# Linear attention with a highway layer: token rows by DMA transposes in the last four steps, seven shared PSUM banks, and a new order of the work

## The chip, the cores and the metric

The kernel runs on one core of one Trainium2 chip. Its time is device microseconds from launch to end. A profile is one profiled execution; it gives a span (first to last recorded work) and that execution's own time, which is a little longer than its span.

The engines are named as in the profile: PE is TensorE (matmuls), with PEld its weight loads; DVE is VectorE; ACT is ScalarE; POOL is GpSimd; SP is SyncE, which here issues nearly all DMAs. Each engine takes its instructions in the order in which they were written, and waits at an instruction whose input is not there yet.

## The reference

Four batches of 768 positions with 8 heads of 64 go through causal linear attention with a decay per head; the result, as 3072 token rows of 512, goes through a highway layer.

```python
for b in range(nb):                       # blocks of 64 positions
    intra = einsum('bhic,bhjc->bhij', qb, kb) * Dmask        # Dmask: lam ** (i - j), 0 above the diagonal
    intra = einsum('bhij,bhjd->bhid', intra, vb)
    inter = einsum('bhid,bhde->bhie', qb * lam_pow, kv_state)
    out[:, :, sl] = intra + inter
    kv_state = lam_block * kv_state + einsum('bhsd,bhse->bhde', kb * rev_pow, vb)
x = out as rows [3072, 512]
H = maximum(x @ w_h, 0);  T = sigmoid(x @ w_t + b_t)
return T * H + (1 - T) * x
```

## The kernel before

The 3072 tokens are worked in 12 steps of 256. A step n is a third of one batch; it has two blocks (0 and 1) of 128 tokens, which lie on partitions 0 to 63 and 64 to 127 of the q, k and v tiles. The decay is put into q (times a power of lam) and into v (times its inverse), so the mask is a plain triangle (`tri`) and the state `kv` only adds up in one PSUM bank of its own.

The work is a list of tokens, `PLAN`. It is the order in which the program is written, and so the order on every engine and in SP's DMA queue; `@DVE`, `@ACT`, `@POOL` choose an engine, the digits behind `=` the PSUM banks. For a step the tokens are:

- `Lq`, `Lk`, `Lv`: loads by SP, two of 256 KB for each. `CQ`, `CK`, `CV`: casts to bf16 with the powers (L231 to L247). `CQ` of either half of the q tile needs both q loads of the step.
- `TQ`, `TK`: q and k turned by TensorE, in eight whole 128x128 transposes each (L264) or in sixteen half ones (L267). `EB`: the result copied from PSUM to `kqT` by ACT or DVE.
- `SP.n.0`, `SP.n.1` (in step 0 `S` and `U`): scores (L285) and state updates (L290). `M`: the mask, four per step, on DVE (L338). `KE`: the state copied out for the next block.
- `I`, `A`: what the state gives (L353) and what the block itself gives (L363), added in one bank; `D` copies it to `xT`, with features on partitions and tokens along the row.
- `XT`: TensorE turns `xT` of both blocks to token rows, eight 128x128 transposes (L375) into one bank, and `XE` copies them to `xr` (L378). `xr` has three buffers.
- The highway layer, per block: `F.n.b.0` is x @ w_h and `F.n.b.1` is x @ w_t (L394, four matmuls of 512 columns each), where `PB` has put the bias into the gate's bank before (L388, ACT). Then `H`: max(h, 0) - x on DVE (L402); `G`: sigmoid on ACT (L407); `X`: the product on DVE (L410); `AD`: plus x, on POOL (L413); `ST`: the store by SP. In step 11 each of these is split into two halves of 256 columns.

`Z` tokens (L428) and `ZT` (L424) are matmuls on zeros, written into banks whose contents nothing reads; they stand where TensorE has little else to do, most of them before the first loads have arrived. The kernel uses eight PSUM banks: one for `kv`, five (`pb`) for all passing results and two (`pt`) for the gates only, which take turns.

Of the kernel before, what the change touches and what calls it, by code (L numbers as in the profile page):

```python
# [22 lines left out]
EB.1.0@ACT D.0.0@ACT Z.5=2 SP.1.0=341 WC.0.0.1@POOL D.0.1@DVE KE.1.0@ACT Z.2=2 I.1.1=0 M.1.0.0@DVE I.1.0=1 CK.2.2@ACT
SP.1.1=2 M.1.1.1@DVE WC.0.1.0@ACT M.1.1.0@DVE Lq.3.0 Lq.3.1 M.1.0.1@DVE TK.2.1=43 A.1.1 A.1.0 CV.2.2@POOL TQ.2.1
XT.0=2 WC.0.0.0@DVE D.1.0@DVE EB.2.0@ACT XE.0@ACT Lk.3.0 Lk.3.1 D.1.1@ACT Lv.3.0 Lv.3.1 WC.1.0.0@POOL F.0.1.0=1 Lk.4.0
KE.1.1@ACT EB.2.1@DVE F.0.0.0=4 H.0.1@DVE WC.1.0.1@ACT WC.1.1.1@ACT Lq.4.1 Lq.4.0 Lk.4.1 Lv.4.1 Lv.4.0 H.0.0@DVE
I.2.0=1 SP.2.0=023 XT.1=4 WC.1.1.0@DVE F.0.1.1 M.2.1.1@DVE F.0.0.1 KE.2.0@ACT M.2.0.0@DVE XE.1@ACT M.2.1.0@DVE
G.0.1@ACT I.2.1=4 CQ.3.2@POOL Lq.5.1 Lq.5.0 Lk.5.0 X.0.1@DVE G.0.0@ACT SP.2.1=0 F.1.0.0=3 M.2.0.1@DVE Lk.6.0 A.2.1
Lk.5.1 Lv.5.1 X.0.0@DVE H.1.0@DVE CK.3.2@POOL A.2.0 Lv.5.0 CV.3.2@POOL PB.1.0@ACT D.2.1@ACT TK.3.0=02 TQ.3.0 D.2.0@DVE
EB.3.1@DVE F.1.0.1 AD.0.0@POOL XT.2=1 PB.2.0@ACT F.2.0.0=2 EB.3.0@DVE SP.3.0=043 G.1.0@ACT XE.2@ACT X.1.0@DVE  # L30
PB.1.1@ACT KE.3.0@ACT F.2.0.1 H.2.0@DVE Lk.6.1 M.3.1.0@DVE Lq.6.1 Lq.6.0 CK.4.2@ACT I.3.1=2 G.2.0@ACT SP.3.1=0
M.3.0.0@DVE CQ.4.2@POOL M.3.1.1@DVE F.2.1.0=1 M.3.0.1@DVE H.2.1@DVE TQ.4.0=43 Lv.6.1 TK.4.0 A.3.1=0 A.3.0 F.1.1.1
KE.3.1@ACT EB.4.0@DVE CV.4.2@POOL EB.4.1@ACT Lk.7.0 Lv.6.0 SP.4.0=341 D.3.1@ACT AD.0.1@POOL D.3.0@DVE X.2.0@DVE
CQ.5.2@POOL M.4.1.0@DVE M.4.1.1@DVE M.4.0.0@DVE XT.3=0 F.3.0.0=2 KE.4.0@ACT AD.2.0@POOL CV.5.2@POOL AD.1.0@POOL
XE.3@ACT F.3.1.0=3 I.4.0=1 I.4.1=0 CK.5.2@ACT H.3.0@DVE SP.4.1=4 F.1.1.0=2 Lq.7.1 Lk.8.1 Lq.7.0 H.3.1@DVE M.4.0.1@DVE
KE.4.1@DVE PB.2.1@ACT G.1.1@ACT CK.6.2@ACT Lv.7.1 TQ.5.0=34 TK.5.0 CQ.6.2@POOL F.2.1.1 EB.5.1@ACT H.1.1@DVE G.2.1@ACT
EB.5.0@DVE X.1.1@DVE PB.3.1@ACT A.4.1 A.4.0 D.4.1@ACT X.2.1@DVE Lk.7.1 SP.5.0=432 F.3.1.1 KE.5.0@ACT D.4.0@ACT
M.5.1.1@DVE G.3.1@ACT TK.6.1=30 TQ.6.1 PB.3.0@ACT Lk.8.0 Lv.7.0 I.5.0=1 M.5.0.0@DVE M.5.1.0@DVE Lq.8.1 I.5.1=4
X.3.1@DVE SP.5.1=2 EB.6.0@ACT PB.4.1@ACT F.3.0.1 M.5.0.1@DVE Lq.8.0 ST.0.1 Lv.8.0 Lq.9.1 Lq.9.0 A.5.1 G.3.0@ACT A.5.0
EB.6.1@DVE AD.1.1@POOL CV.6.2@POOL D.5.1@ACT Lk.9.0 CQ.7.2@POOL SP.6.0=023 X.3.0@DVE Lq.10.1 Lv.8.1 D.5.0@ACT  # L40
PB.4.0@ACT CK.7.2@POOL F.4.1.1 ST.0.0 M.6.1.0@DVE M.6.1.1@DVE M.6.0.0@DVE ST.1.0 Lq.10.0 XT.4=1 AD.2.1@POOL F.4.1.0=0
CV.7.2@POOL Lk.10.1 Lk.10.0 Lv.9.1 G.4.1@ACT ST.2.0 Lk.9.1 TK.7.0=24 KE.6.0@ACT TQ.7.0 XE.4@ACT H.4.1@DVE I.6.1=3
EB.7.1@DVE SP.6.1=1 X.4.1@DVE AD.3.1@POOL AD.3.0@POOL F.4.0.1 XT.5=0 Lv.9.0 F.4.0.0=4 CQ.9.2@POOL CQ.8.2@POOL
CK.8.2@ACT G.4.0@ACT EB.7.0@ACT M.6.0.1@DVE XE.5@DVE A.6.1=1 A.6.0 D.6.0@ACT CV.8.2@POOL D.6.1@ACT H.4.0@DVE
KE.6.1@DVE F.5.1.0=0 X.4.0@DVE AD.4.0@POOL PB.5.1@ACT PB.6.1@ACT SP.7.0=142 KE.7.0@ACT XT.6=3 XE.6@ACT H.5.1@DVE
F.5.1.1 M.7.0.0@DVE M.7.1.0@DVE M.7.1.1@DVE I.7.1=2 I.7.0=0 SP.7.1=1 F.6.1.0=3 M.7.0.1@DVE TK.8.0=14 G.5.1@ACT TQ.8.0
F.6.1.1 X.5.1@DVE A.7.1 EB.8.1@DVE KE.7.1@ACT PB.5.0@ACT H.6.1@DVE A.7.0 EB.8.0@ACT AD.4.1@POOL ST.4.0 G.6.1@ACT
SP.8.0=314 D.7.1@ACT D.7.0@ACT F.5.0.1 X.6.1@DVE M.8.0.0@DVE M.8.1.0@DVE KE.8.0@ACT PB.6.0@ACT M.8.1.1@DVE F.5.0.0=2
AD.5.1@POOL I.8.0=4 Lv.11.0 I.8.1=3 SP.8.1=0 F.6.0.1 ST.1.1 Lv.10.0 Lv.10.1 M.8.0.1@DVE G.5.0@ACT CK.9.2@ACT
CK.10.2@ACT CV.9.2@POOL H.5.0@DVE X.5.0@DVE A.8.1 A.8.0 TQ.9.0=20 D.8.1@DVE AD.5.0@POOL Lk.11.1 ST.3.0 Lk.11.0  # L50
D.8.0@ACT TK.9.0 F.6.0.0=1 EB.9.1@ACT XT.7=3 ST.2.1 EB.9.0@DVE SP.9.0=204 G.6.0@ACT PB.8.0@ACT XE.7@ACT H.6.0@DVE
X.6.0@DVE XT.8=1 F.8.0.1 ST.3.1 F.8.0.0=3 M.9.0.0@DVE M.9.1.0@DVE XE.8@ACT CQ.10.2@POOL M.9.1.1@DVE KE.9.0@DVE
# [428 lines left out]
```

## Time and profile before

| | |
|---|---|
| time, median of 3 runs | 103.66 us (103.03 to 103.72) |
| profiled execution, its own time | 104.03 us |
| its span | 102.3 us |
| busy: PE / DVE / ACT / POOL | 91.1 / 81.2 / 75.2 / 76.0 us |
| granted TensorE clock | 0.998 |
| moved by DMA | 27.56 MB, 269 GB/s over the span |

In a list of windows each row is a stretch of the span in us, its length, and then for PE, PEld, DVE, ACT and POOL the busy time with the number of instructions; behind them the granted clock, the share of time in which the 16 DMA engines were busy, and GB/s. The chain of waits has a start, a duration, an engine, the tile that is written and a line. A group of instructions has its line, engine, operation, tiles, shapes and count, then busy time and mean ns of one, then the engine's idle time before them and what ended it. Busy times of an engine's neighbouring instructions overlap a little, so that four masks in a row took 2.49 us, about 620 ns each, where their mean is 684.

### The profile page before, as it was taken

The numbers are of one execution on the slowest core, as the hardware profiler recorded it, in microseconds if no ns is written. First come the engines' busy times: TensorE is split into PE (matmuls) and PEld (weight loads), VectorE is DVE, ScalarE is ACT, GpSimd is POOL, SyncE is SP. The second block draws the span as 40 slices with busy tenths as digits, with TensorE's granted clock in tenths as the row PEclk, the third lists the DMA queues.
The fourth block names the chain that finished last, engine by engine and source line by source line (L and its number), as shares of the span: only waits on it lengthen the run. The fifth ranks groups of instructions, "written<-read, shape, count | busy, mean of one in ns | idle before, by whom it ended". The sixth has DMA issues, their size and how long they took to land.

```text
span 102.3 us, 4447 instructions
## 1 busy us (share of the span) xinstructions
PE 91.1 (89%) x1883; PEld 56.2 (55%) x1907; DVE 81.2 (79%) x143; ACT 75.2 (73%) x124; POOL 76.0 (74%) x67
## 2 busy tenths in 40 slices
...
GB/s 8 255 294 357 347 360 366 375 397 351 281 286 345 334 285 290 258 347 331 302 342 267 373 333 330 314 243 274 357 378 245 68 143 103 109 2 148 252 272 55
DMA packets 36870, 27.56 MB, mean 269 GB/s; under 512 B 1777, under 2 KB 33009, under 8 KB 36850
## 3 DMA queue, kind: packets, MB, share of 16 engines
...
q10 hardware_dynamic: 146, 0.01, 0.1%
...
## 4 chain that ended last, share of the span: by engine, by line
PE 74%; DVE 11%; ACT 6%; issue 4%; POOL 0%; DVEq 0%; POOLq 0%
PE pt L394 18%; PE pb L394 18%; PE pb L285 7%; PE pb L428 6%; DVE m L338 6%; PE pb L363 6%; PE pb L375 5%; PE pb L353 5%; PE pb L267 5%; ACT xr L110 2%; ACT kqT L110 2%; PE kv L290 2%; PE pb L264 1%; DVE gx L410 1%; ACT pt L407 1%
## 5 line engine op out<-in xcount | busy, mean ns | idle before, releaser
L338 DVE TENSOR_TENSOR m<-pb,tri 128x512 bf16<-128x512 f32 x48 | 30.7, 684 | 5.2 <-PE pb L285 4.5
L239 POOL TENSOR_TENSOR qb<-qf,pow_q 128x1024 bf16<-128x1024 f32 (+1 forms) x13 | 22.6, 1747 | 11.4 <-DMA qf<-in_q_dram 9.9
L413 POOL TENSOR_TENSOR o<-gx,xr 128x512 f32<-128x512 bf16 x22 | 25.3, 1156 | 7.4 <-DVE gx L410 6.0
L394 PEld LDWEIGHTS <-xT 128*128 128x128 bf16 x208 | 18.1, 98 | 15.5 <-issue 0.4
L394 PE MATMUL pt<-w_b,xT 128*128 128x512 bf16 (+1 forms) x90 | 23.5, 361 | 1.5 <-issue 0.6
L394 PE MATMUL pb<-w_b,xT 128*128 128x512 bf16 (+1 forms) x97 | 23.7, 362 | 0.5 <-issue 0.2
L246 POOL TENSOR_TENSOR vs<-vf,pow_v 128x1024 bf16<-128x1024 f32 x10 | 19.1, 1905 | 1.8 <-DMA vf<-in_v_dram 1.2
L407 ACT ACTIVATE pt<-pt 128x512 f32<-128x512 f32 (+1 forms) x26 | 14.4, 554 | 4.5 <-PE pt L394 4.3
L410 DVE TENSOR_TENSOR gx<-pt,hm 128x512 bf16<-128x512 f32 x22 | 15.1, 687 | 3.2 <-ACT pt L407 2.7
L388 ACT ACTIVATE pt<-bt_all 128x512 f32<-128x512 f32 x24 | 14.4, 604 | 3.7 <-DVE gx L410 3.6
L402 DVE SCALAR_TENSOR_TENSOR hm<-pb,xr 128x512 bf16<-128x512 f32 x22 | 15.0, 685 | 2.0 <-ACT xr L110 1.8
L110 ACT ACTIVATE kqT<-pb 128x1024 bf16<-128x1024 bf16 x12 | 12.3, 1024 | 4.7 <-PE pb L264 3.4
L285 PE MATMUL pb<-kqT 64*64 64x128 bf16 x384 | 14.4, 220 | 0.6 <-DVE kqT L112 0.3
L285 PEld LDWEIGHTS <-kqT 64*64 64x64 bf16 x384 | 11.2, 105 | 2.3 <-ACT xT L110 0.8
L110 ACT ACTIVATE xr<-pb 128x1024 bf16<-128x1024 bf16 x11 | 11.2, 1024 | 1.6 <-PE pb L375 1.4
L290 PE MATMUL kv<-vs,kb 64*64 64x64 bf16 x320 | 11.8, 193 | 0.0
L110 ACT ACTIVATE xT<-pb 128x512 bf16<-128x512 f32 x18 | 10.2, 595 | 1.3 <-PE pb L363 1.3
L290 PEld LDWEIGHTS <-kb 64*64 64x64 bf16 x320 | 9.8, 107 | 0.4 <-issue 0.4
L428 PE MATMUL pb<-blank,id 128*128 128x512 bf16 x28 | 8.9, 467 | 0.2 <-issue 0.2
L363 PE MATMUL pb<-m,vs 64*64 64x128 bf16 x384 | 7.9, 219 | 1.1 <-issue 0.6
L363 PEld LDWEIGHTS <-vs 64*64 64x64 bf16 x384 | 6.0, 106 | 5.3 <-issue 5.0
L112 DVE COPY kqT<-pb 128x1024 bf16<-128x1024 bf16 x12 | 8.1, 683 | 0.4 <-PE pb L267 0.3
...
## 6 DMA issues: line engine op xcount, KB each, us to landing
...
w_f<-in_moe_w_h_dram SPq DMA_DIRECT2D x2, 512.0 KB, 6.9
w_f<-in_moe_w_t_dram SPq DMA_DIRECT2D x2, 512.0 KB, 8.0
out_dram<-oh SPq DMA_DIRECT2D x4, 128.0 KB, 2.4
lam_all<-in_lam_dram ACTq DMA_DIRECT2D x1, 4.0 KB, 3.1
```

Of the source, the lines that this page charges most:

```text
L110: A.activation(dst, src, AF.Copy)
L239: ENG[eng].tensor_tensor(new(("qb", n), [128, 4, 4, D])[:, :, ys], in0=get("qf", n)[:, ys].rearrange("p y (i d) -> p i y d", i=4), in1=pow ...
L246: ENG[eng].tensor_tensor(new(("vs", n), [128, H, J, D])[:, hs], in0=get("vf", n)[:, hs].rearrange("p h (j d) -> p h j d", j=J), in1=pow_v[ ...
L285: T.matmul(get("s", n, e, hp // 2)[half(b), hp % 2, j, :], lhsT=keys(n, e, hp, j, b), rhs=queries(n, e, hp, b), start=True, stop=True)
L290: T.matmul(kv[half(e), hp], lhsT=get("kb", n)[half(b), j, 2 * hp + e, :], rhs=get("vs", n)[half(b), 2 * hp + e, j, :], start=first, stop=T ...
L338: V.tensor_tensor(new(("m", n, e, u), [128, 2, J, C]), in0=get("s", n, e, u), in1=tri[:, None].to_broadcast([128, 2, J, C]), op=ALU.mult)
L363: T.matmul(get("o", n, b)[half(e), hp, :], lhsT=get("vs", n)[half(b), 2 * hp + e, j, :], rhs=get("m", n, e, u)[half(b), hp % 2, j, :], sta ...
L394: T.matmul(t, lhsT=get("xT", n, b)[:, kc, :], rhs=w_b[w][:, kc, cs], start=(w == 0 and kc == 0), stop=(kc == KC - 1), skip_group_check=boo ...
L407: A.activation(t, t, AF.Sigmoid)
L410: V.tensor_tensor(small("gx", n, b, p), in0=get("t", n, b)[:, cols(p)], in1=get("hm", n, b, p), op=ALU.mult)
L413: ENG[eng].tensor_tensor(small("o", n, b, p, F32), in0=get("gx", n, b, p), in1=get("xr", n)[:, b, cols(p)], op=ALU.add)
L428: T.matmul(banks[bk[0]], lhsT=id128, rhs=blank, start=True, stop=True)
```

## The change

For steps 8 to 11 the tokens `XT` and `XE` are gone. In their place `XD.n.b` has SP issue a DMA that transposes `xT` of one block (128x512 bf16, 128 KB) straight into `xr`, eight DMAs in all. Steps 0 to 7 still use TensorE. The two gate banks are gone as banks of their own: seven `pb` banks serve all results and the gates, and `PB` names a bank. The `o` tiles, which wait for their store, are twelve instead of eight, and `kqT` has three buffers instead of two. The scores' matmuls open a bank only with the first of a half, which changes no instruction's size. Step 0's q and k are turned in half transposes rather than whole ones (steps 1, 2 and 6 keep whole ones). `PLAN` is a new list: the same operations but for those named, in another order, some on other engines.

```diff
-BUFS = dict(kf=5,qf=5,vf=5,kb=3,qb=3,vs=3,kqT=2,m=8,xT=6,xr=3,hm=4,gx=4,hmh=4,gxh=4,ss=4,o=8,oh=4,tb=2)
+BUFS = dict(kf=5,qf=5,vf=5,kb=3,qb=3,vs=3,kqT=3,m=8,xT=6,xr=3,hm=4,gx=4,hmh=4,gxh=4,ss=4,o=12,oh=4)
...
-    banks = [ps.tile([128, 512], F32, name=f"pb{i}") for i in range(5)]
-    gates = [ps.tile([128, DM], F32, name=f"pt{i}") for i in range(2)]
+    banks = [ps.tile([128, 512], F32, name=f"pb{i}") for i in range(7)]
...
+    def turn_dma(n, b):
+        nc.sync.dma_start_transpose(out=new(("xr", n), [C, 2, DM])[:, b].rearrange("p (j f) -> p j f", f=128),
+                                    in_=get("xT", n, b).rearrange("p j t -> p (j t)"))
...
-    def preset(n, b):
-        made["t", n, b] = gates[gate_turn[0] % 2]
-        gate_turn[0] += 1
-        A.activation(get("t", n, b), bt_all, AF.Copy)
+    def preset(n, b, bk):
+        A.activation(bank(("t", n, b), bk[0], [C, DM]), bt_all, AF.Copy)
...
+        "XD": lambda a, e, bk: turn_dma(*a),
-        "XT": lambda a, e, bk: turn(*a, bk), "XE": lambda a, e, bk: evac_x(*a, e), "PB": lambda a, e, bk: preset(*a),
+        "XT": lambda a, e, bk: turn(*a, bk), "XE": lambda a, e, bk: evac_x(*a, e), "PB": lambda a, e, bk: preset(*a, bk),
```

Of the list, the first line and the line where the last step's `XD` stands show what kind of change it is:

```diff
-Lq.0.0 Lk.0.0 ZT Z.11=3 B=0 Lq.0.1 Lk.0.1 Lv.0.0 Lv.0.1 CQ.0.1@POOL Lq.1.0 Lv.1.1 CK.0.0@DVE CK.0.1@POOL Lq.1.1
+Lq.0.1 Lq.0.0 CQ.0.1@POOL CQ.0.0@POOL Lk.0.0 Lk.0.1 CK.0.0@DVE ZT Z.6=6 TQ.0.0=01 Lv.0.0 Lv.0.1 CK.0.1@ACT Lq.1.0
...
+F.10.0.0=3 PB.10.1@ACT=5 PB.11.0@ACT=0 F.10.1.0=1 F.10.1.1 H.10.0@DVE G.10.1@ACT ST.8.0 ST.7.0 ST.6.1 XD.11.1
```

The start, on POOL and after the constants. `qb` is the cast q, `kb` the cast k, `vs` the cast v; `qf_69` is q of step 0 and `qf_70` q of step 1. Before:

```order
L239 TENSOR_TENSOR qb_170<-qf_69,pow_q 128x4x128
L112 CAST kb_174<-kf_64 128x4x2x64
L239 TENSOR_TENSOR qb_184<-qf_70,pow_q 128x4x128 x2
L112 CAST kb_241<-kf_65 128x4x2x64
L239 TENSOR_TENSOR qb_337<-qf_71,pow_q 128x1024
```

And now:

```order
L238 TENSOR_TENSOR qb_156<-qf_69,pow_q 128x4x128 x2
L238 TENSOR_TENSOR qb_265<-qf_70,pow_q 128x4x128
L112 CAST kb_307<-kf_65 128x4x2x64
L238 TENSOR_TENSOR qb_265<-qf_70,pow_q 128x4x128
L245 TENSOR_TENSOR vs_317<-vf_75,pow_v 128x512 x2
```

Both halves of the first q are now cast on POOL, one after the other, where DVE had one; the second half of k of step 0 goes from POOL to ACT, and v of step 1 from DVE to POOL.

The end, on DVE, from the last mask (`m`) on. `hm`/`hmh` are `H`, `gx`/`gxh` are `X`, `oh` is an `AD` of half a row, `xT` is `D`. Before, where `xr_647` is step 10 and `xr_819` step 11:

```order
L338 TENSOR_TENSOR m_483<-pb_145,tri 128x512
L402 SCALAR_TENSOR_TENSOR hm_568<-pb_146,xr_647 128x512
L410 TENSOR_TENSOR gx_663<-pt_148,hm_568 128x512
L402 SCALAR_TENSOR_TENSOR hm_577<-pb_146,xr_647 128x512
L410 TENSOR_TENSOR gx_698<-pt_149,hm_577 128x512
L402 SCALAR_TENSOR_TENSOR hmh_2457<-pb_146,xr_819 128x256
L402 SCALAR_TENSOR_TENSOR hmh_2459<-pb_143,xr_819 128x256
L410 TENSOR_TENSOR gxh_2475<-pt_148,hmh_2459 128x256
```

And now, where `xr_570` is step 9, `xr_590` step 10 and `xr_855` step 11:

```order
L344 TENSOR_TENSOR m_492<-pb_153,tri 128x512
L401 SCALAR_TENSOR_TENSOR hm_648<-pb_149,xr_570 128x512
L409 TENSOR_TENSOR gx_788<-pb_151,hm_648 128x512
L401 SCALAR_TENSOR_TENSOR hm_650<-pb_148,xr_570 128x512
L112 CAST xT_782<-pb_152 128x512
L409 TENSOR_TENSOR gx_963<-pb_147,hm_650 128x512
L401 SCALAR_TENSOR_TENSOR hm_595<-pb_150,xr_590 128x512
L409 TENSOR_TENSOR gx_685<-pb_153,hm_595 128x512
L401 SCALAR_TENSOR_TENSOR hm_606<-pb_148,xr_590 128x512
L401 SCALAR_TENSOR_TENSOR hmh_2461<-pb_150,xr_855 128x256
L409 TENSOR_TENSOR gx_743<-pb_152,hm_606 128x512
```

Behind the last mask DVE had the `H` and `X` of step 10 and the halves of step 11; now it has those of step 9 too, and one `D` of step 11.

SP's queue, late. `out_dram<-o` is a store, `DMA_TRANSPOSE` an `XD`. Before, the last rows are stores only:

```order
L416 DMA out_dram<-o_83 128x512
L416 DMA out_dram<-o_86 128x512
L416 DMA out_dram<-o_82 128x512
L416 DMA out_dram<-o_84 128x512
L416 DMA out_dram<-oh_87 128x256
```

And now, from the transposes of step 10 to those of step 11:

```order
L380 DMA_TRANSPOSE xr_590<-xT_564 128x4x128
L380 DMA_TRANSPOSE xr_590<-xT_554 128x4x128
L415 DMA out_dram<-o_83 128x512
L415 DMA out_dram<-o_81 128x512
L415 DMA out_dram<-o_79 128x512
L380 DMA_TRANSPOSE xr_855<-xT_779 128x4x128
L380 DMA_TRANSPOSE xr_855<-xT_782 128x4x128
L415 DMA out_dram<-o_85 128x512
```

Three stores (of `AD.8.0`, `AD.7.0`, `AD.6.1`) stand ahead of the two transposes of step 11, and the rest of the stores behind them.

More of the change, by code (lines that the diff above doesn't have):

```diff
@@ L23 @@
[L23 to L52, printed above, removed]
```

96 lines of the change are left out of this document (62 added, 34 removed).

## The prediction

> **What bounds the kernel now.** I read the page's first part, the chain of waits, and then busy time in windows cut where the work changes.
>
> ```profile
> PE 91.1 (89%) x1883; PEld 56.2 (55%) x1907; DVE 81.2 (79%) x143; ACT 75.2 (73%) x124; POOL 76.0 (74%) x67
> PE 74%; DVE 11%; ACT 6%; issue 4%; POOL 0%; DVEq 0%; POOLq 0%
> 0.00:9.60 9.60, 8.17 (x24) 2.92 (x25) 4.29 (x15) 4.35 (x7) 4.17 (x13) 1.00 0.74 219
> 9.60:17.10 7.50, 6.16 (x146) 4.58 (x147) 5.85 (x11) 4.04 (x6) 2.61 (x3) 1.00 1.11 356
> 17.10:25.40 8.30, 7.37 (x201) 5.45 (x203) 6.89 (x12) 6.15 (x10) 5.79 (x5) 1.00 1.08 375
> 25.40:89.98 64.58, 61.91 (x1435) 38.25 (x1452) 57.27 (x94) 54.43 (x89) 56.86 (x39) 1.00 0.88 276
> 89.98:97.80 7.82, 7.50 (x84) 4.98 (x84) 5.80 (x13) 5.86 (x12) 5.91 (x6) 1.00 0.43 161
> 97.80:102.30 4.50, 0.00 (x0) 0.00 (x0) 1.14 (x3) 0.37 (x1) 0.67 (x1) 0.96 0.38 133
> ```
>
> In the long middle (25.40 to 89.98) PE is busy 61.91 of 64.58 us, and the chain is 74% PE: less work for PE is time there, as long as nobody else takes over. DVE is next with 57.27 (89%). The middle has 2.67 us of PE idling to win at most. Before 25.40 PE waits for others; after 97.80 it has ended.
>
> ```profile
> 9.73 0.91 PE pb L264 x16
> 11.90 0.44 PE pb L285 x13
> 12.43 0.67 DVE m L338
> 16.44 0.61 DVE kqT L112
> 17.10 0.22 PE pb L285 x2
> 29.25 0.57 PE pb L267 x32
> 81.76 0.86 PE pt L394 x4
> 87.88 0.45 PE pb L375 x8
> 89.76 0.23 PE pb L285 x6
> 90.95 0.57 PE pb L363 x32
> 97.33 0.45 PE pt L394 x4
> 97.80 0.38 ACT pt L407
> 98.20 0.44 DVE gxh L410
> 98.66 0.43 DVE oh L413
> ```
>
> These pieces of the chain give the prices on PE: q and k of a step turned whole 0.91 us (x16) or in halves 0.57 (x32), a block of the highway layer 0.86, `XT` 0.45, an intra pair 0.57, half a block 0.45. They also give the marks: first scores at 11.90, step 1's first scores at 17.10, the last scores' end at 89.98 (T below), the last matmul's end at 97.78, the last `AD`'s end at 99.09. The last store and the end take 102.30 - 99.09 = 3.21.
>
> **The change part by part. Sums first.** Without `XT` in four steps PE loses 4 x 0.45 = 1.80, and without the whole transposes of step 0 another 0.34. What the other engines lose or get:
>
> ```profile
> L338 DVE TENSOR_TENSOR m<-pb,tri 128x512 bf16<-128x512 f32 x48 | 30.7, 684 | 5.2 <-PE pb L285 4.5
> L402 DVE SCALAR_TENSOR_TENSOR hm<-pb,xr 128x512 bf16<-128x512 f32 x22 | 15.0, 685 | 2.0 <-ACT xr L110 1.8 <-PE pb L394 0.2
> L410 DVE TENSOR_TENSOR gx<-pt,hm 128x512 bf16<-128x512 f32 x22 | 15.1, 687 | 3.2 <-ACT pt L407 2.7
> L402 DVE SCALAR_TENSOR_TENSOR hmh<-pb,xr 128x256 bf16<-128x256 f32 x4 | 1.6, 418 | 0.2 <-ACT xr L110 0.2
> L410 DVE TENSOR_TENSOR gxh<-pt,hmh 128x256 bf16<-128x256 f32 x4 | 1.7, 425 | 0.6 <-ACT pt L407 0.3
> L112 DVE CAST xT<-pb 128x512 bf16<-128x512 f32 x6 | 4.1, 684 | 0.9 <-PE pb L363 0.9
> L112 DVE COPY xr<-pb 128x1024 bf16<-128x1024 bf16 x1 | 0.7, 681 | 0.0
> L110 ACT ACTIVATE xr<-pb 128x1024 bf16<-128x1024 bf16 x11 | 11.2, 1024 | 1.6 <-PE pb L375 1.4
> L110 ACT ACTIVATE kb<-kf 128x1024 bf16<-128x1024 f32 x7 | 7.3, 1065 | 0.0
> L413 POOL TENSOR_TENSOR o<-gx,xr 128x512 f32<-128x512 bf16 x22 | 25.3, 1156 | 7.4 <-DVE gx L410 6.0
> ```
>
> ACT had eleven `XE` and keeps four: -7 x 1.024 = -7.2, and takes over two casts of k (+2 x 1.065) and a few smaller ones, so it gets lighter by 5 at most. DVE goes from one `XE` to four (+2.0) and loses casts of q and v at the start and one `D`: about zero. So PE gets 2.1 lighter and DVE does not, which is what a rival below rests on.
>
> **The start.** Loads are issued in another order.
>
> ```profile
> 1.57 0.59 SPq L222 DMA_DIRECT2D kf<-in_k_dram  x1
> 2.21 0.61 SPq L220 DMA_DIRECT2D qf<-in_q_dram  x1
> 5.46 0.43 DVE L112 CAST kb<-kf 128x512 bf16<-128x512 f32 x1 [0.49 <-DMA kf<-in_k_dram]
> 6.83 1.56 POOL L239 TENSOR_TENSOR qb<-qf,pow_q 128x512 bf16<-128x512 f32 x1 [3.97 <-DMA qf<-in_q_dram]
> 8.45 1.64 DVE L246 TENSOR_TENSOR vs<-vf,pow_v 128x512 bf16<-128x512 f32 x2 [0.97 <-DMA vf<-in_v_dram]
> 11.36 2.06 POOL L239 TENSOR_TENSOR qb<-qf,pow_q 128x512 bf16<-128x512 f32 x2 [2.42 <-DMA qf<-in_q_dram]
> ```
>
> The second load issued (k, at 1.57) landed at 5.46, the third (q, at 2.21) at 6.83, 4.6 us after its issue. Both halves of q are now first and second, so there at 5.5 to 6.1. POOL casts them in a row, 2.06 at best and 1.56 + 1.03 at worst: 7.6 to 8.7. Turning q and k in halves takes PE 0.57, ACT's copy 1.02 (as `xr` above), some spins: first scores at 9.7 to 10.4, not 11.90. Most of it is lost again. v of step 0 is scaled on DVE behind its copy (9.3 to 10.0, plus 1.28 to 1.64: 10.6 to 11.6), the state waits for v, and the first mask for the state's copy and the bias matmul: 12.9 to 13.5, where it was 12.43. DVE then has a cast of k (0.43), two masks and the copy of step 1 (0.61 to 0.68) ahead of step 1's first scores, which so come at 16.0 to 16.7, not 17.10: a lead of 0.4 to 1.1. I take 0.8, the 0.34 included, and that it lasts through the fill, where the new list does two more blocks before step 2's scores and comes there later by about their price.
>
> **The middle.** Three of the four lost `XT` lie before T: 3 x 0.45 = 1.35 (one lies behind T in the list before). Sharing seven banks, the third `kqT` and twelve `o` tiles add no instruction. The `o` tiles can save little: POOL's idling before `AD` is 6.0 of 7.4 us for DVE. What sharing does to PE's idling the trace cannot show; from below the bound is that all 2.67 us go, from above that PE idles as it does in 17.10:25.40, 0.93 of 8.30 or 11%, on some 61 us: 6.8, so 4.1 more. I take no change, the nearest row being the middle itself. For the first time a gate can hold up scores and the other way round, and behind a waiting mask stand the `H` and `X` of two other steps.
>
> **The end.** In the new list two blocks of step 9 and a fourth of step 10 stand behind the last scores. PE behind T, before: 3 x 0.86 + 0.57 + 0.45 + 8 x 0.45 = 7.20; now 6 x 0.86 + 0.57 + 8 x 0.45 = 9.33. The three blocks, 2.58, were ahead of T and make it earlier: T = 89.98 - 0.80 - 1.35 - 2.58 = 85.25. Behind T, DVE is the longer one: nine operations of 0.685 and ten halves of 0.42 to 0.43 behind the last mask, where it had four and nine. Put one behind the other (0.65 and 0.42 each, as they overlap) with each one's matmuls checked off: mask done at T + 0.9, `D.11.0` at T + 3.6, `H.10.0` from T + 4.2, when its block ends (T + 2.3 + 2 x 0.86), `H.11.0.0` from T + 6.2, again when its matmuls end, then 0.65 + 10 x 0.42 = 4.85 without a gap to the last `AD` at T + 11.0; PE's last matmul ends at T + 9.3. The end is T + 11.0 + 3.21 = T + 14.2, where it was T + 12.3.
>
> **The transposes.** No row shows one. Eight must land before an `H` reads `xr`. For steps 8 to 10 the `H` stands 4 or more DVE operations behind, and the transposes wait for the `AD` of three steps before (the buffer). Step 11 is the tight one: `XD.11.0` goes out when `D.11.0` ends, T + 3.6, and is wanted at T + 6.2. Bounds for its landing:
>
> ```profile
> out_dram<-oh SPq DMA_DIRECT2D x4, 128.0 KB, 2.4
> w_f<-in_moe_w_t_dram SPq DMA_DIRECT2D x2, 512.0 KB, 8.0
> ```
>
> 2.4 us is the same 128 KB, in the same stretch, where the DMA engines are busy 0.43 of the time; 8.0 is the worst median of a load, in full traffic. The first is the nearer in size and place. Up to 2.6 us nothing moves; each us beyond is a us at the end, as DVE has no gap behind it. I take nothing; at 8.0 it is 5.4. Three stores of 256 KB stand ahead in SP's queue, but wait only for `AD.8.0`, done near T. What stands behind a waiting transpose in that queue are stores, and behind `XD.8.0` the last load, `Lv.11.0`. POOL wants it for `CV.11.2`, but has a cast and three `AD` (3 x 1.156 = 3.5 us) between; at nothing, unless `D.8.0` or `AD.5.0` come that much late.
>
> **Sum.** 85.25 + 14.2 = 99.45 of span, against 102.3; the execution's own time is 104.03, 1.73 over its span, so 101.2. The runs' median is 0.37 below that execution: **100.8 us**.
>
> **The rivals.**
>
> *DVE or the banks take over.* PE's loss turns into idling: DVE's work is unchanged and its share of the middle already 89%, masks wait for PE (4.5 us) and `X` for ACT (2.7). For it: 2.1 us off PE alone. Against: DVE too has about 4 us less before T, moved behind it. With 1.8 to 4.1 us more idling: 102.6 to 104.9.
>
> *The transposes are slow; the result is slower.* `XD.11.0` at the upper row, 8.0, lands at T + 11.6; behind it DVE still has 4.85 us, then 3.21: T + 19.7, 5.4 more, 106.2. It decides against the change from 5.5 us on, where the 2.9 won are gone. For it: no row. Against: 128 KB in light traffic.
> One way to get there is that a transpose of 128x512 goes as four 128x128 pieces in a row and the second DMA behind the first. Issued at T + 2.7 and with the upper row for both together, `XD.11.0` lands at T + 10.7, giving 105.3. The Trainium skill ("VectorE: DVE Perf Modes", The three transpose paths) speaks for such a case: it gives 1309 ns for one 128x128 by DMA and 390 ns on TensorE, and advises TensorE where PSUM will do. By its figure two DMAs of four pieces would take 10.5 us, an estimate, and the time be about 108.
>
> *The idling goes.* Shared banks and the third `kqT` take most of the 2.67 us: 98.1 to 99.4.
>
> **How the numbers follow.** The forecast, idling within 1.5 us of now: 99.4 to 102.6, chance 0.54. Idling gone 0.11. DVE or banks 0.19, of which half stays below 104.7. Slow transposes 0.16, most of it above 104.5. About 1%, or 1.0 us, is what can be told from no change here. Faster (below 102.6): 0.54 + 0.11 = 0.65. Same (102.6 to 104.7): 0.14. Slower: 0.21. The range 98.8 to 104.8 leaves out some 0.05 below and 0.15 above; the forecast's own is 99.4 to 102.6.
>
> **What would show it.** In the profile after: first scores near 10, step 1's at 16 to 16.7; PE busy about 2 us less, with 2.7 us of idling in the middle; last scores' end near 85, last matmul near 94.6, last `AD` near 96.2; DMA rows for `xr<-xT` near 2.4 us, and no `H` that waits for a DMA. Wrong if `H` rows wait for such a DMA, if the middle's idling has grown by 2 us or more, or if step 1's scores come after 17.1.

## The result and the profile after

The changed kernel takes 103.18 us, the median of 20 runs (101.46 to 105.46), beside 103.44 us of the kernel before in 20 runs on the same chip (102.61 to 105.12). The ratio is 0.989, interval 0.985 to 0.9931: 1.1% faster, where 2.8% was forecast. Like every ratio below it counts only undisturbed runs, of the changed kernel eight of the 20, with a median of 102.14 us (so the medians of all runs lie closer together), while the profiles of `xt11`, `xtall2`, `before7b`, `kq2`, `nospin`, `best1` and `best2` are of disturbed ones. The changed kernel's profiled execution has a span of 100.3 us and a time of its own of 102.49.

The first part of its page, the chain's shares, and busy time in windows cut as in the prediction (the fourth ends at the last scores, T; the fifth with the last matmul):

```profile
PE 91.0 (91%) x1891; PEld 54.3 (54%) x1891; DVE 80.8 (81%) x143; ACT 72.2 (72%) x123; POOL 74.2 (74%) x64
...
PE 75%; DVE 7%; ACT 6%; DMA 5%; SPq 2%; issue 1%; ACTq 0%; DVEq 0%
```

```profile
0.00:9.60 9.60, 6.69 (x48) 2.69 (x49) 2.98 (x13) 3.01 (x6) 4.11 (x13) 1.00 0.69 204
9.60:17.10 7.50, 7.50 (x108) 3.88 (x106) 5.47 (x10) 3.50 (x5) 5.03 (x6) 1.00 1.08 344
17.10:25.40 8.30, 8.05 (x193) 5.60 (x192) 7.21 (x14) 6.52 (x14) 5.01 (x4) 1.00 1.08 381
25.40:85.30 59.90, 58.98 (x1458) 36.40 (x1458) 54.48 (x89) 53.72 (x91) 54.25 (x37) 1.00 0.99 292
85.30:95.58 10.28, 9.77 (x88) 5.69 (x88) 8.54 (x17) 5.11 (x11) 4.91 (x5) 1.00 0.78 253
95.58:100.30 4.72, 0.00 (x0) 0.00 (x0) 2.10 (x5) 0.37 (x1) 0.94 (x2) 0.79 0.48 172
```

PE is busy nearly without a gap from 9.6 us to T: it idles 0.92 us in the middle, where before showed 2.67. PE is still what bounds the middle. Behind T the last matmul ends at T + 10.3, and 4.7 us more pass until the end.

The marks, from the chain of waits of the changed kernel:

```profile
10.24 0.35 PE pb L291 x13
...
14.78 1.02 PE pb L263 x16
15.80 1.51 PE pb L423 x7
17.31 0.15 PE pb L291
...
85.08 0.22 PE pb L291 x6
...
97.33 0.42 DVE oh L412
```

The first scores come at 10.24 (before: 11.90), step 1's first scores at 17.31 (before: 17.10), the last scores end at 85.30 (before: 89.98), the last `AD` ends at 97.75, and 2.55 us later everything is done.

### The profile page after: what moved, and what is told of

It reads as the page before. It is cut to its first block, busy times and chain, and to the rows that moved or that the text cites. A ratio compares the mean times of both kernels' runs of the same rounds, so it can differ in the third digit from the quotient of the medians.

```text
span 100.3 us, 4427 instructions
## 1 busy us (share of the span) xinstructions
PE 91.0 (91%) x1891; PEld 54.3 (54%) x1891; DVE 80.8 (81%) x143; ACT 72.2 (72%) x123; POOL 74.2 (74%) x64
## 4 chain that ended last, share of the span: by engine, by line
PE 75%; DVE 7%; ACT 6%; DMA 5%; SPq 2%; issue 1%; ACTq 0%; DVEq 0%
PE pb L393 40%; PE pb L291 8%; PE pb L362 5%; DMA kf<-in_k_dram 5%; DVE m L344 5%; PE pb L423 5%; PE pb L352 5%; PE pb L266 4%; PE kv L296 3%; PE pb L263 2%; PE pb L374 2%; ACT kqT L110 2%; ACT pb L406 2%; SPq L219 1%; DVE gxh L409 1%
## 5 line engine op out<-in xcount | busy, mean ns | idle before, releaser
L393 PE MATMUL pb<-w_b,xT 128*128 128x512 bf16 (+1 forms) x208 | 46.6, 364 | 0.5 <-ACT pb L406 0.4
L238 POOL TENSOR_TENSOR qb<-qf,pow_q 128x1024 bf16<-128x1024 f32 (+1 forms) x14 | 23.2, 1657 | 7.3 <-DMA qf<-in_q_dram 6.5
L245 POOL TENSOR_TENSOR vs<-vf,pow_v 128x1024 bf16<-128x1024 f32 (+1 forms) x12 | 21.2, 1773 | 2.7 <-DMA vf<-in_v_dram 1.8
L406 ACT ACTIVATE pb<-pb 128x512 f32<-128x512 f32 (+1 forms) x26 | 14.1, 550 | 5.4 <-PE pb L393 4.3
L409 DVE TENSOR_TENSOR gx<-pb,hm 128x512 bf16<-128x512 f32 x22 | 15.0, 684 | 1.1 <-ACT pb L406 0.3
L387 ACT ACTIVATE pb<-bt_all 128x512 f32<-128x512 f32 x24 | 14.1, 601 | 0.9 <-DVE m L344 0.5
L110 ACT ACTIVATE xT<-pb 128x512 bf16<-128x512 f32 x19 | 10.9, 594 | 2.7 <-PE pb L362 2.6
L110 ACT ACTIVATE kb<-kf 128x1024 bf16<-128x1024 f32 (+1 forms) x10 | 10.1, 1010 | 3.1 <-DMA kf<-in_k_dram 3.1
L110 ACT ACTIVATE ss<-kv 128x256 bf16<-128x256 f32 x17 | 6.5, 382 | 1.7 <-PE pb L291 1.0
L423 PE MATMUL pb<-blank,id 128*128 128x512 bf16 x26 | 7.3, 420 | 0.0
```

What stands on the lines that cost most here:

```text
L110: A.activation(dst, src, AF.Copy)
L238: ENG[eng].tensor_tensor(new(("qb", n), [128, 4, 4, D])[:, :, ys], in0=get("qf", n)[:, ys].rearrange("p y (i d) -> p i y d", i=4), in1=pow ...
L245: ENG[eng].tensor_tensor(new(("vs", n), [128, H, J, D])[:, hs], in0=get("vf", n)[:, hs].rearrange("p h (j d) -> p h j d", j=J), in1=pow_v[ ...
L393: T.matmul(t, lhsT=get("xT", n, b)[:, kc, :], rhs=w_b[w][:, kc, cs], start=(w == 0 and kc == 0), stop=(kc == KC - 1), skip_group_check=boo ...
L406: A.activation(t, t, AF.Sigmoid)
L409: V.tensor_tensor(small("gx", n, b, p), in0=get("t", n, b)[:, cols(p)], in1=get("hm", n, b, p), op=ALU.mult)
```

## The experiments

All times are compared with the kernel before on the same chip; a ratio of 0.989 is that of the changed kernel. Where a diff is shown, tokens are those of the plan: `XT` and `XE` turn x on TensorE and copy it out, `XD` is the transfer that turns, `Z.n` are n filler matmuls, `G` sigmoid, `X` gate product, `AD` add.

### What each part is worth: transposes, banks, tiles, order

**Only step 11 back on TensorE** (`xt11`).

```
- XD.11.1 ... XD.11.0
+ F.10.0.1 XT.11=2 ... G.10.0@ACT XE.11@ACT
```

> The changed kernel, but step 11 alone turns x on TensorE again (8 transposes into bank 2 behind F.10.0.1, 0.45 us, copied by ACT, 1.02 us, which idles there). Theory (in step 11 the DMA costs more than the transposes): DVE no longer waits for a DMA, PE gets 0.45 longer behind the last scores, H.11.0.0 starts at about 92.1 instead of 92.57: 0.2 to 0.5 us less than the changed kernel, ratio 0.984 to 0.987. Rival (behind the last scores PE sets the end): 0.45 us more, ratio 0.993.

Ratio 1.0035 [0.9976, 1.0094]: the whole gain is gone with this one step, 1.0035 / 0.989 = 1.015, or 1.5 us. `XT` itself is 0.45 us on PE. Neither the theory nor the rival had so much. Behind T, in the timeline of `xt11`:

```profile
92.56 0.62 PE L374 MATMUL pb<-id,xT 128*128 128x128 bf16 x8 [0.40 <-DVE xT L112]
...
93.26 1.02 ACT L110 ACTIVATE xr<-pb 128x1024 bf16<-128x1024 bf16 x1 [0.42 <-issue]
...
94.19 1.11 ACT L387 ACTIVATE pb<-bt_all 128x512 f32<-128x512 f32 x2
```

PE waits 0.40 us for x, and ACT copies for 1.02 us ahead of the two bias presets of the last blocks. The last `AD` ends at T + 13.24 instead of T + 12.45, so these waits account for 0.8 us (T here is 88.78). Where the rest of the 1.5 us is lost isn't shown; the two intervals leave room for it to be less.

**All four steps back on TensorE in the new order**, once with `XT.10` ahead of the last intra pairs (`xtall`), once behind them, so that no preset waits for `XE.10` (`xtall2`).

```
- XD.8.1 XD.8.0 ... XD.9.0 XD.9.1 ... XD.10.1 XD.10.0 ... XD.11.1 XD.11.0
+ XT.8=4 XE.8@ACT ... XT.9=6 XE.9@ACT ... XT.10=2 XE.10@ACT ... XT.11=1 XE.11@ACT
```

> The changed kernel with all four XD pairs given back to TensorE (XT.8 to XT.11 into free banks, XE on ACT): the order, the seven banks and the twelve tiles stay. Theory of the prediction (PE sets the middle, an XT costs its 0.45 us): against the run with step 11 alone given back 3 x 0.45 = 1.35 us more, ratio 0.997 to 1.000. Rival (PE's work in steps 8 to 10 is not what the middle waits for, and the copies go to an ACT with room): within 0.4 us of the run with step 11 alone, ratio 0.985 to 0.990; then the DMA transposes bring nothing and the new order brings it all.

> All four XD pairs given back to TensorE, as in the run before, but with XT.10 behind A.11.0 and XE.10 behind D.11.1 on ACT: there the copy of step 10 stood ahead of a gate's preset, PE waited 1.3 us for the preset and DVE 2.4 us for PE, and T (the end of the last scores) was 86.14 against 85.30, that is 0.84 us for two XT. Theory (an XT costs 0.45 us each, no more, if nothing waits for its copy): T again 0.8 to 0.9 later, two more behind T, less the wait of 0.83 us for the DMA: 0.9 to 1.4 us more than the changed kernel, ratio 0.998 to 1.003. Rival (the copies on ACT and the banks have no room in this order, the DMAs bring more than the sum of the XT): 2.5 us more or above, ratio 1.013 or above.

1.0366 [1.0301, 1.0431] and 1.021 [1.0141, 1.0279]. In `xtall` T is 86.15, 0.85 later than in the changed kernel for the two `XT` that lie ahead of it, 0.42 each: the price of 0.45 holds. The tails are longer, the last `AD` at T + 15.1 and T + 14.1. So both theories, which added up the `XT` alone, were too low, and for `xtall2` the rival's 1.013 or more came true. In the new order, with the copies placed as here, the transposes by DMA are worth 3%: the new order with TensorE turning is slower than the kernel before.

**The transposes alone in the old order** (`before_xd`).

```
- XT.8=1 ... XE.8@ACT        (and so for 9, 10, 11)
+ XD.8.0 XD.8.1
```

> The kernel before with one part of the change alone: in steps 8 to 11 XD in the place of XT, and no XE; its order, its five banks and two gate banks and its eight o tiles stay. Theory of the prediction (PE sets the middle, an XT is worth 0.45 us): T at 88.6 instead of 89.98, and behind T the waits of DVE for the copied x (0.2 and 1.8 us in all) turn into a wait for a DMA: XD.11 goes out at T + 2.6 and T + 3.9, lands at T + 6.5, where H.11 started at T + 5.0; so 0 to 1.4 us less, ratio 0.987 to 1.000. Rival (the transposes wait in SP's queue behind stores that wait for POOL, 18.7 us of such waits in its trace): 1 us or more slower, ratio above 1.01.

Six runs took 106.31 to 112.37 us, beside 102.84 to 105.02 of before: even the fastest of the six is slower than the slowest of before. SP's queue does hold up the last loads, which in the old order stand behind `XD.8`. The queue and GpSimd's cast of the last q, in this kernel:

```profile
69.86 3.08 SPq L381 DMA_TRANSPOSE xr<-xT  x2
...
73.63 0.42 SPq L222 DMA_DIRECT2D vf<-in_v_dram  x1
...
79.51 1.90 POOL L239 TENSOR_TENSOR qb<-qf,pow_q 128x1024 bf16<-128x1024 f32 x1 [2.75 <-DMA qf<-in_q_dram]
```

and the same load of v in the kernel before:

```profile
70.10 0.48 SPq L222 DMA_DIRECT2D vf<-in_v_dram  x1
```

Two transposes hold the queue 3.1 us, the last loads go out 3.5 us later, and POOL waits 2.75 us for q. In the new order all loads but `Lv.11.0` are ahead of the first `XD`. But this delay is not what sets the time of this execution, the fastest of the six: from 66 us to the end its chain of waits holds no DMA and nothing of POOL. T is 90.71, where a start 0.45 later and three lost `XT` would have made it 89.98 + 0.45 - 1.35 = 89.1. Most of these 1.6 us are lost in the last stretch ahead of T, where the chain leaves PE for ACT and DVE:

```profile
86.20 0.38 ACT ss L110
86.59 0.99 ACT xT L110 x2
87.58 1.27 DVE m L338 x2
...
88.89 1.02 PE pb L398 x4
```

The windows of that stretch, from the end of step 10's intra pairs to T, here and then in the kernel before:

```profile
85.50:90.71 5.21, 4.57 (x78) 2.47 (x75) 3.63 (x6) 3.05 (x7) 2.23 (x3) 1.00 0.21 37
85.56:89.98 4.42, 4.37 (x86) 2.64 (x76) 3.74 (x6) 3.70 (x8) 1.00 (x1) 1.00 0.34 122
```

With `XT.10` gone the stretch is 0.8 us longer, not 0.45 shorter, and PE idles 0.64 us in it instead of 0.05. So in the old order PE's saving turns into waiting for ACT and DVE, which is the prediction's first rival. Behind T another 1.1 us is lost: the last `AD` ends at T + 10.2 instead of T + 9.1. What makes the other five runs longer still isn't shown.

**Seven shared banks alone**, in the old order (`before7`, `before7b`): five plus two banks become one pool, each group taking the bank that has been free longest. In `before7` gates were given banks last turned into and lost their bias; `before7b` has none of that, at the price of less choice.

> The kernel before, in its own order and with TensorE turning every step, with one thing changed: the five working banks and the two gate banks are one pool of seven, and each group takes the bank that has been free longest. Theory (sharing brings nothing by itself, because the order before was written around five and two): the same as before within 1%, ratio 0.99 to 1.01, that is 102.5 to 104.5 us where before takes 103.5. Rival (the waits for banks were what the new kernel removed, and the order only follows): ratio 0.985 or less, with PE's idling between 25.4 and 85 us falling from 2.6 us to about 1 us, as in the new kernel.

> The kernel before, in its own order and with TensorE turning every step, whose five working banks and two gate banks are one pool of seven; a bank that was last turned into is not given to a gate, whose bias would be written over there otherwise (in the first such kernel it was: five to nine gates of the 24 lost their bias, with the same instructions). Theory (sharing brings nothing without an order written for it): within 1% of before or slower, ratio 0.99 to 1.02; PE's idling from 25.4 to 85 us falls from 2.6 us to about 1.5, and what it gains comes back behind the last scores. Rival (sharing is the gain): ratio 0.985 or less.

1.0136 [1.0042, 1.0231] and 1.0266 [1.0144, 1.0387], each from two runs: slower, and not the rival's gain. In `before7`, window 25.40 to 85:

```profile
25.40:85.00 59.60, 58.07 (x1337) 35.19 (x1335) 52.90 (x87) 49.82 (x82) 54.97 (x38) 1.00 0.92 290
```

PE idles 1.53 us, where before's profile shows 2.62 for the same window, and yet T is 90.93, later than before's 89.98. The row also points to a flaw in the prediction's reading. Before's profile has 208 weight loads for the blocks but 155 + 32 matmuls; `before7b`, with the same work, has 176 + 32 and more busy time in them. From the groups by form, before and then `before7b`:

```profile
L394 PE MATMUL pb<-w_b,xT 128*128 128x512 bf16 x81 | 21.5, 380 | 0.5 <-issue 0.2
L394 PE MATMUL pt<-w_b,xT 128*128 128x512 bf16 x74 | 21.1, 380 | 1.3 <-issue 0.6
...
L394 PEld LDWEIGHTS <-xT 128*128 128x128 bf16 x208 | 18.1, 98 | 15.5 <-issue 0.4
```

```profile
L393 PE MATMUL pb<-w_b,xT 128*128 128x512 bf16 x176 | 43.6, 380 | 0.1
```

21 matmul records are missing before, and by this comparison 43.6 - 42.6 = 1.0 us of busy time with them. So up to about 1 us of the 2.67 us of idling was not idling, an estimate: with all 176 the changed kernel, in its own order, shows 42.8. Nor did sharing by itself take away PE's idling, as 2.62 - 1.0 = 1.6 is what `before7` has.

**Fewer tiles in the new order.** `bufs` has eight output tiles instead of twelve and two pairs of kqT instead of three; `kq2` only the two pairs. With eight tiles three adds (`AD.4.0`, `AD.5.1`, `AD.5.0`) take a tile whose content isn't stored yet, so these stores write another block.

```
- kqT=3, ... o=12
+ kqT=2, ... o=8        (kq2: kqT=2, o=12)
```

> The changed kernel with eight output tiles instead of twelve and two pairs of kqT instead of three, everything else as it is. Theory (the order puts the stores late and leans on the twelve tiles): GpSimd's adds wait for stores that stand behind loads in SP's queue, the casts behind them on GpSimd come late, and the time rises by 1 to 4 us (ratio to the changed kernel 1.01 to 1.04). Rival (the extra tiles were only convenient): within 0.5 us of the changed kernel, ratio to before 0.985 to 0.995.

> The changed kernel with two pairs of kqT instead of three, everything else as it is. Theory (the third pair only lets a copy run ahead at a few places): within 0.5 us of the changed kernel, ratio to before 0.985 to 0.998. Rival (the order leans on it as it does on the output tiles): copies wait for scores and intra matmuls, 1 us or more slower than the changed kernel, ratio 1.0 or more.

`bufs`: 1.1264 [1.1176, 1.1352], some 13 us, where 1 to 4 were expected. One wait makes nearly all of it, GpSimd's for a store:

```profile
POOL o L412 <- DMA out_dram<-o: 12.9, 1, 12.9
...
PE pb L266 <- POOL qb L238: 11.7, 2, 11.2
```

Casts of q stand behind that add on GpSimd, and PE's transposes wait for them. The twelve tiles cost no instruction and save none, but the new order, which stores late, rests on them. `kq2` takes 103.18 us in the median (101.07 to 105.66), the changed kernel beside it 104.04 (101.92 to 106.1): no loss without the third pair is to be seen.

### The end

**The two transfers of step 11 exchanged** (`swap`).

```
- XD.11.1 F.11.0.0.0=3 ... F.11.1.0.1=1 XD.11.0
+ XD.11.0 F.11.0.0.0=3 ... F.11.1.0.1=1 XD.11.1
```

> The changed kernel with one thing moved: XD.11.0 is issued ahead of XD.11.1. In the trace of the changed kernel a transposing DMA holds SP for 1.2 to 1.3 us and lands 2.6 us after that; XD.11.1 is issued at 88.72, XD.11.0 behind it at 89.97 although its input is there at 89.02, and DVE waits 0.83 us for it at H.11.0.0 (92.57). Theory (the second issue in SP's queue is late): XD.11.0 goes out at about 89.3, lands at about 91.9, the wait falls from 0.83 to 0.2, the gate operations behind it shift with it, and the time is 0.6 to 0.8 us less than the changed kernel's, ratio to the kernel before 0.981 to 0.983 against 0.989. Rival (the end is set by the gate's bank: G waits for X, and a matmul for G): no more than 0.2 us, ratio 0.987 to 0.991.

0.9925 [0.986, 0.999]: the 0.6 to 0.8 us of the theory did not come, and the kernel is not told apart from the changed one. First the changed kernel, where SP's queue, the first half `H` and the gate products read:

```profile
88.72 2.52 SPq L380 DMA_TRANSPOSE xr<-xT  x2
...
92.57 0.42 DVE L401 SCALAR_TENSOR_TENSOR hmh<-pb,xr 128x256 bf16<-128x256 f32 x1 [0.83 <-DMA xr<-xT]
...
94.29 0.65 ACT L406 ACTIVATE pb<-pb 128x256 f32<-128x256 f32 x2 [0.81 <-DVE gxh L409]
94.69 0.42 DVE L409 TENSOR_TENSOR gxh<-pb,hmh 128x256 bf16<-128x256 f32 x1 [0.43 <-ACT pb L406]
...
94.98 0.60 PE L393 MATMUL pb<-w_b,xT 128*128 128x256 bf16 x4 [0.41 <-ACT pb L406]
```

The first transfer, `XD.11.1`, holds the queue until 89.97; `XD.11.0` goes out behind it, and `H.11.0.0` waits 0.83 us for it. In `swap` that wait is gone, and the first half `H` and the last add are these:

```profile
91.47 0.42 DVE L401 SCALAR_TENSOR_TENSOR hmh<-pb,xr 128x256 bf16<-128x256 f32 x1
...
96.74 0.42 DVE L412 TENSOR_TENSOR oh<-gxh,xr 128x256 f32<-128x256 bf16 x1
```

With T = 85.04 that is T + 6.43 instead of T + 7.27, but the last add ends at T + 12.12 instead of T + 12.45. Of 0.84 us 0.33 arrives. The rest is lost in the gate's bank: a sigmoid waits for the product that reads the other half of its bank, and TensorE's next half block for the sigmoid behind it.

**The transfer without the turning** (`plain`): the same bytes, copied.

```
- nc.sync.dma_start_transpose(out=...xr..., in_=...xT...)
+ nc.sync.dma_start(out=...xr..., in_=...xT...)
```

> The changed kernel in which the eight transfers from xT to xr are plain copies of the same 128 KB and do not transpose: x of steps 8 to 11 is left unturned, so the output of these steps is another one; the work and the order of everything else are the same. Theory (turning costs SP's queue and the landing little more than moving): each holds SP about 0.6 us instead of 1.2, lands 2.0 to 2.6 us after its issue, XD.11.0 lands about 0.7 to 1.2 us earlier behind the last scores, and H.11.0.0 stands 6.4 us behind them instead of 7.3; span 0.3 us shorter or less. Rival (turning is what is slow): landing 1.5 us or less, and a span shorter by 1 us or more.

The changed kernel's transfers, then those of `plain` (time that each holds SP's queue in ns as minimum, median, maximum; and us from issue to landing):

```profile
L380 SPq DMA_TRANSPOSE xr<-xT x8: 1188/1225/1337, 69.5 to 90.0; - x8
...
DMA to landing us min/median/max: 2.4/2.6/4.4
```

```profile
L380 SPq DMA_DIRECT2D xr<-xT x8: 470/490/602, 69.2 to 89.0; - x8
...
DMA to landing us min/median/max: 2.0/2.1/4.3
```

Turning 128 x 512 costs 0.73 us more of the queue and 0.5 us more of landing. Here that is worth as much as the exchange: the last add at T + 12.12, span 99.9, in one execution. The Trainium skill's 1309 ns for one 128x128 ("VectorE: DVE Perf Modes", The three transpose paths) would give four such pieces about 5.2 us, an estimate; the whole 128 x 512 landed in 2.6 us, so the measurement decides against it.

**Another order behind T** (`tail`): the exchange, all half blocks in one go on TensorE, each sigmoid ahead of the product that reads the other half of its bank.

```
- H.11.0.1 X.11.0.0 ... G.11.0.1 X.11.0.1 H.11.1.1 G.11.1.1 F.11.1.0.0=2 F.11.1.1.0 ... AD.11.0.0@DVE
+ F.11.1.0.0=6 F.11.1.1.0 H.11.0.1 G.11.0.1 X.11.0.0 ... X.11.0.1 H.11.1.1 G.11.1.1 ... AD.11.0.0@POOL
```

> The changed kernel with another order behind the last scores: XD.11.0 ahead of XD.11.1; all eight block halves of step 11 in one go on TensorE, the h of block 11.1.0 in bank 6 instead of bank 2; each sigmoid ahead of the gate product that reads the other half of its bank; both first adds on GpSimd. Theory (what the tail lost against the forecast is waits for a half-used gate bank and for the transfer): PE idles no more between 93.5 and 95 us, the last matmul is at T + 9.3 or earlier instead of T + 10.3 (T is the end of the last scores), the last add at T + 11.2 to 11.8 instead of 12.45, the span 0.7 to 1.2 us shorter and the ratio to before 0.977 to 0.983, 0.6 to 1.1% below the changed kernel on the same chip. Rival (the tail is VectorE's and GpSimd's work, and moves with its sum alone): the last add at T + 12 or later, no difference of more than 0.3 us.

0.9861 [0.977, 0.9953]; the changed kernel beside it, unchanged (`again`):

> The changed kernel once more, unchanged, beside the other three on the same chip, so that they are compared with it and not only with before. Theory: ratio to before 0.985 to 0.993, as it was. Rival (the gain differs by chip): outside 0.98 to 0.998.

0.9892 [0.9825, 0.9959], as in its first comparison. The end of `tail` in its timeline, and one window of it:

```profile
93.14 0.77 ACT L406 ACTIVATE pb<-pb 128x256 f32<-128x256 f32 x2 [1.23 <-PE pb L393]
...
95.63 0.76 DVE L409 TENSOR_TENSOR gxh<-pb,hmh 128x256 bf16<-128x256 f32 x2 [0.27 <-ACT pb L406]
...
96.42 0.66 DVE L412 TENSOR_TENSOR oh<-gxh,xr 128x256 f32<-128x256 bf16 x1
```

```profile
94.00:96.00 2.00, 0.79 (x8) 0.46 (x5) 1.73 (x6) 0.74 (x2) 1.51 (x3) 1.00 1.06 406
```

The mechanism is as expected: the sigmoids go in pairs, the last matmul ends at 94.79, T + 9.45 (T = 85.34), the last add ends at T + 11.74, where it is T + 12.46 in `again`. But the span of this execution is 100.9, that of `again` 100.5: the last stores end 3.8 us behind the add instead of 2.7. The DMA engines move 406 GB/s in the window in which these stores are issued, but 379 in the same window of `again`, so why the stores end so late stays open; the other three executions of `tail` behind its ratio have spans of 99.8 to 100.2. By the ratios the time moved by 0.3%, less than the intervals.

### The start

**Fillers taken away or added.** `nospin` has no `Z.7` ahead of step 1's scores; `fill` has `Z.8` for `Z.6` and `Z.2` more between the first transposes; `best1` is `swap` with the fillers of `fill` and `Z.4` for `Z.7` (its expectation names only the last); `best2` is `best1` with `Z.12` for `Z.8`; `final` is the start of `best2` and the end of `tail`.

```
- ZT Z.6=6 TQ.0.0=01 Lv.0.0 ... BC@ACT Z.7=4 SP.1.0=561
+ ZT Z.12=6 TQ.0.0=01 Z.2=6 Lv.0.0 ... BC@ACT Z.4=4 SP.1.0=561      (best2, final)
```

> The changed kernel without the seven filler matmuls (Z.7) ahead of step 1's first scores. In its trace the copied q and k of step 1 are there at 16.53, but the fillers hold PE until 17.31. Theory (the lost lead of the start is these fillers, and PE sets all behind it): step 1's scores at 16.6 and 0.5 to 0.7 us less than the changed kernel, ratio 0.982 to 0.985. Rival (step 2 waits for loads, weights and casts whatever step 1 does): scores of step 1 earlier, those of step 2 still at 25.5, ratio 0.987 to 0.991.

> The changed kernel with four more filler matmuls at the start: Z.8 for Z.6 ahead of TQ.0.0, and Z.2 between TQ.0.0 and TK.0.0, where PE waits 0.89 us for q and 0.59 us for k. In the profile of the run without Z.7 the last k load of step 0 landed at 9.0 instead of 8.1, PE idled until then, and the granted clock from 10 to 15 us was 0.69. Theory (PE idling at the start lets the granted clock fall, and the changed kernel has less filler there): the mean granted clock of every execution is 0.985 or more, the widest spread of times (101.5 to 105.5) shrinks to about 1.5 us, and the median of all executions falls by about 1 us to some 102; the ratio of undisturbed executions stays at 0.987 to 0.990. Rival (late loads alone make the spread): clocks between 0.97 and 1.00 as before, and the same spread.

> The changed kernel with XD.11.0 ahead of XD.11.1 and four instead of seven fillers ahead of step 1's first scores. Theory: the end gains what the run with the two transposes exchanged gained behind the last scores (H.11.0.0 at T + 6.5 instead of T + 7.3, last AD at T + 12.1 instead of T + 12.4, its trace), and step 1's scores come at 16.7 instead of 17.3: 0.3 to 0.9 us less than the changed kernel, ratio 0.980 to 0.986. Rival (the gate's bank and step 2's loads hold both ends): ratio 0.987 to 0.991.

> The changed kernel with three edits at its ends: XD.11.0 ahead of XD.11.1; four fillers instead of seven ahead of step 1's scores; and at the start twelve fillers instead of six behind the first bias presets and two between the transposes of q and k, so that PE does not idle while the first q and k land. Theory (the clock falls in the changed kernel's longer executions because PE idles at the start): PE is busy about 8 of the first 9.6 us as before (6.7 now), every execution's mean clock is 0.985 or more, and the median comes to 101.5 to 102.5 us, ratio to before 0.975 to 0.985. Rival (the longer executions have late loads and the clock follows from something else): mean clocks still spread down to 0.97 or lower, ratio 0.985 to 0.995 as the changed kernel.

> The changed kernel with the start of the run with more fillers (twelve instead of six behind the first presets, two between the first transposes, four instead of seven ahead of step 1's scores) and the end of the run with the other order of the last blocks. Theory (the two ends are independent, each worth about 0.3 to 0.6 us of the span): T at 84.8 to 85.4, the last add at T + 11.8, ratio to before 0.977 to 0.984. Rival (the fillers cost PE what they save, and the stores take back what the tail gains): ratio 0.985 to 0.992, as the changed kernel.

0.9921 [0.9861, 0.9981], 0.9885 [0.9807, 0.9964], 0.9781 [0.9686, 0.9876], 0.9886 [0.9841, 0.993] and 0.9925 [0.9873, 0.9976]. The theories of `nospin`, `best2` and `final`, which asked for 0.985 or less, missed. None but `best1` is told apart from the changed kernel, and that barely and by two executions; `best2`, which differs from it by four more fillers, is at 0.9886. So no better version is shown, and the two repairs together (`final`) add up to nothing that can be measured.

In two profiles the clock falls at the start. In `kq2` k of step 0 lands late (its second cast starts at 8.40 us instead of 8.08), PE idles 0.9 of the 2 us from 8 to 10, and from 10 to 12.5 us the granted clock is 0.50; in `nospin` it is the same, with k at 9.02. Windows of `kq2`, then its fillers and first scores:

```profile
8.00:10.00 2.00, 1.11 (x21) 0.53 (x18) 0.56 (x1) 1.22 (x2) 0.00 (x0) 0.88 1.04 341
10.00:12.50 2.50, 2.50 (x22) 0.94 (x21) 1.33 (x3) 1.71 (x2) 1.05 (x1) 0.50 1.12 340
```

```profile
9.31 2.15 PE L423 MATMUL pb<-blank,id 128*128 128x512 bf16 x5
...
11.39 0.64 PE L291 MATMUL pb<-kqT 64*64 64x128 bf16 x16
```

Five fillers take 2.15 us there and 1.25 in the changed kernel's own profile, and the first scores come at 11.4. With twelve fillers the lowest mean clock of an execution is a little higher, 0.977 (`best2`) and 0.980 (`final`), than the 0.971 of the changed kernel and 0.968 of `again`, but below the 0.985 that `best2`'s theory named. The ratio did not move, and one execution of `best2` took 105.08 us at a mean clock of 0.995. So it isn't shown that a low clock at the start costs the changed kernel its time.

## Why the prediction was wrong

The direction, the price of an `XT` and the range held; the size did not: 2.8% was forecast, 1.1% measured. The forecast of 100.8 us is 1.34 below the 102.14 us of the runs behind the ratio. Its own sum shows where, term by term:

- T: forecast 85.25, measured 85.30. No error in sum, by errors that cancel (below), so this is luck.
- **The end behind T, the step that failed most:** forecast T + 14.2, measured T + 15.0: 0.8 us. `XD.11.0` was to go out at T + 3.6 and the ten halves to run without a gap to the last `AD` at T + 11.0. It went out at T + 4.67, behind its twin in SP's queue, and the last `AD` ended at T + 12.45.
- What lies outside the span: taken as 1.73 from before, 2.19 in the changed kernel's execution: 0.46 us.
- From one execution to the runs: I subtracted 0.37, since before's execution stood 0.37 above its median. The changed kernel's stands 0.35 above (102.49 against 102.14). That it fits is luck too, as one execution of one kernel says nothing about the next kernel.

0.05 + 0.8 + 0.46 + 0.02 = 1.33. A second error sits in the base: by the ratio the kernel before takes 102.14 / 0.989 = 103.3 us, not the 103.66 of three runs, so 0.4 us of the forecast gain of 103.66 - 100.8 = 2.86 were never there to win. Without both errors 1.1 us are left, as measured. The spans of the two profiled executions mislead as well: they differ by 102.3 - 100.3 = 2.0 us.

Point by point:

**The start.** First scores at 9.7 to 10.4: they came at 10.24. Step 1's first scores at 16.0 to 16.7: they came at 17.31, and the prediction named a value past 17.1 as a sign that it is wrong. The copies they need were done in time, but I had not counted the fillers on PE. The changed kernel's rows:

```profile
15.39 1.02 ACT L110 ACTIVATE kqT<-pb 128x1024 bf16<-128x1024 bf16 x1 [3.98 <-PE pb L263]
15.63 1.67 PE L423 MATMUL pb<-blank,id 128*128 128x512 bf16 x7
15.84 0.69 DVE L112 COPY kqT<-pb 128x1024 bf16<-128x1024 bf16 x1
```

Both copies end by 16.53; the seven fillers hold PE until 17.31. The lead was -0.2 instead of +0.8. With four fillers (`best2`) the scores came at 16.7, and the time did not follow, so the lead is not worth what I gave it.

**The middle.** Three `XT` at 0.45: right, 0.42 each by `xtall`. "PE's idling stays as it is": wrong, but by less than the rows say. 0.92 us is left of 2.67, of which up to about 1 us was missing records, so the true change is between 0.75 and 1.75. What the start lost by the wrong lead, 1.0 us, the fill and the middle gave back: from step 1's first scores to T it is 85.30 - 17.31 = 67.99 us, where the forecast had 89.98 - 17.10 - 1.35 - 2.58 = 68.95. So T was right by two errors that cancel. The rival "the idling goes" fits these rows, but its time, 98.1 to 99.4, did not come. Which of the banks, the tiles and the order removed the idling was not separated; sharing alone makes the old order slower.

**The end.** `H.11.0.0` from T + 6.2 on: it came at T + 7.27, because of an 0.83 us wait for the transfer, and an `H` that waits for such a DMA was another sign that the prediction named. The landing was right, 2.6 us against 2.4, and so was `D.11.0`, done at T + 3.7 against T + 3.6. What was missing is the 1.2 us that a transpose holds SP's queue, twice in a row: `XD.11.1` held it until 89.97, T + 4.67. I had checked what stands ahead in the queue, stores, but not that the other transfer of the same step does. The other part is the gate's bank: the two halves of a block share one, which I had taken as ten operations "without a gap". Of the 1.45 us by which the last `AD` is late, the exchange alone wins back 0.33 (`swap`), the exchange with another order 0.71 (`tail`, T + 11.74); the remaining 0.74 was not traced further. The last store and the end took 2.55 instead of 3.21, which hides 0.66 us of this error in the span.

**The rivals.** "The transposes are slow" fell: 2.6 us landing, not 8. In its place stands the price that no row of before could show, the queue. "DVE or the banks take over" fell for the new order, where PE idles less than before and bounds the middle; in the old order (`before_xd`) it is what the chain shows.
